# Attention and a gated MLP on one core: combined weights for all 768-token blocks are made in the plain blocks

## The chip, the cores and the metric

The kernel runs on one core of one Trainium2 chip. The time is the device time of one execution in microseconds (us), and lower is better. Five engines work beside each other: TensorE (PE, matmuls; PEld is its weight load), VectorE (DVE), ScalarE (ACT), GpSimd (POOL), and SyncE (SP), which issues nearly all transfers. Each engine takes its own instructions in the order that was fixed when the program was built, and waits on semaphores for the others.

## The reference

```python
k_p = k.reshape(B, H, Sp, pool, D).mean(axis=3)        # 576 keys pooled to 72
v_p = v.reshape(B, H, Sp, pool, D).mean(axis=3)
scores = scale * np.matmul(q, k_p.transpose(0, 1, 3, 2))
attn = softmax(scores)
x = np.matmul(attn, v_p)                               # then (B*S, H*D) = 4608 x 512
h = x @ w_in                                           # 512 -> 2048
g = h * np.clip(h + 3.0, 0.0, 6.0) / 6.0
out = g @ w_out                                        # 2048 -> 512
```

Batch and heads are 8 each, head size is 64, all in float32. Every float32 operand of a large matmul is split into a high and a low part in a reduced type (`hi` is a rounding copy on ACT, `lo = x - hi` on DVE), and a product is three matmuls: hi·hi, hi·lo and lo·hi.

## The kernel before

**Blocks.** The 4608 tokens are cut into blocks (`BLOCKS`): 512, 256, 384 and 384 tokens, and then eight of 384 that are taken two at a time, as four blocks of 768. The first four (blocks 0 to 3) are "plain", the four others use a product scheme with seven block products in place of eight. Attention for a later block runs in small steps ("slots") between the matmuls of an earlier one, so that its PE work is spread over all stages.

**A plain block** (`run`, class `Step`) has 16 steps, one for each 128 of the 2048 hidden columns. Step u does the 12 matmuls of h (L847), then ACT's relu (L855), DVE's `gate` (L859), ACT's `ghi` (L863) and DVE's `glo` (L867), then the `out` products (L878) of step u - 2, three per 128 tokens, and last the hooks of u: calls listed in a table `hooks[block][u]`. The h sums alternate between two PSUM banks, so h of step u + 2 waits for gate of step u. The buffer `g` exists once, so relu of a step waits for `glo` of the one before. All weights are in SBUF in these blocks, each in its own place: tile `w_f` holds the two parts of w_in and w_out of step f. The places lie in two pools, `consts[0]` for f under 8 and `consts[1]` for the others.

**A 768-token block** (`super_block`) treats h as a 2 x 2 block product: x (two token halves by two halves of the 512 columns) times pairs of w_in tiles, done by seven products per pair (`N1`, L1140). Its operands are sums of blocks. The sums of x are made by `x_ops` (eleven makes, each with one DVE operation at L1044 or L1052). The sums of w_in are the same for all tokens: `sums_of(i, h)` makes them once for pair i of 8, in two halves h of 128 columns, in `hooks[2]` and `hooks[3]` at every second step, into a tile `wq` of which there is one buffer; they are stored to DRAM (`w_dram`, shown as wd) by SP. `plain_of` stores the weights that go in as they are (24 stores to wd, 32 to `w2_dram`, shown as w2d); its calls stand in the hooks of blocks 2 and 3, but nothing holds them there.

The weights then stream back for each 768-token block in chunks of 512 KB through two rings, wsFalse and wsTrue (`chunk`, L998). The ring wsFalse lies in the pool `late0`, which takes the place of `consts[0]` at step 9 of block 3 (`swap`); wsTrue lies in `late2`, which takes the place of the pool that holds `wq`, at the last step of block 3 (`more`).

The out part of the second, third and fourth 768-token block (`SEVEN = (1, 2, 3)`) is done by seven products too (`out_seven`, L1267): 28 rounds, each of 18 matmuls of 256 columns. The first does it plainly (`out_plain`, L1194), 16 rounds of 18 matmuls of 512 columns, and beside it `combine` makes the sums of w_out for the others from the chunks that pass (per pair: two adds L1023, four mixes L1026, one ACT copy L1028, one subtraction L1029) and stores them to `w2t_dram` (w2t, L1032).

**What sets the order.** For the first stretch (to step 3 of block 1) the order on every engine is a written table, `ORDER`. Behind it a planner orders the instructions of each engine by a simulated time, in the order of the program among those that it thinks ready. Two helpers bind it: `behind(a, b)` keeps a after b on one engine, with no wait, and `after_mark()` keeps the instruction just written behind the last marked one on its engine; on DVE in plain blocks that is `glo`. Both set only the earliest place. `CUTS` is the share of the attention steps of a 768-token block that goes to its h part, the rest goes to its out part.

Of the kernel before, what the change touches and what calls it, by code (L numbers as in the profile page):

```python
# [8 lines left out]
F32 = mybir.dt.float32  # L9
F32R = mybir.dt.float32r  # L10
# [88 lines left out]
def attention_moe_kernel(  # L99
# [506 lines left out]
    def x_tile(j, name, dtype):  # L606
        if (j, name) not in xs:
            if name == "x":
                xs[j, name] = pool.tile([P, NCC, TMAX], dtype, name=name, bufs=2)
            else:  # L610
                xs[j, name] = early_x[-1].tile(
                    [P, NCC, max(BLOCKS) if j < 2 else TMAX], dtype, name=name, bufs=1
                )
        return xs[j, name][:, :, : BLOCKS[j]]
# [324 lines left out]
    def sums_of(i, h):  # L939

        half = slice(h * P, (h + 1) * P)
        t = early_x[-1].tile([P, 2, 4, P], F32, name="wq", bufs=1)
        hi, q = t[:, 0], t[:, 1]
        for r, w in enumerate(pair_of(i)):
            nc.vector.tensor_tensor(
                out=q[:, 2 * r : 2 * r + 2], in0=w[:, 0, :, half], in1=w[:, 1, :, half], op=ALU.add
            )
            after_mark()
        for to, a, b, how in ((0, 0, 2, ALU.subtract), (2, 2, 3, ALU.add), (3, 3, 0, ALU.subtract), (1, 1, 3, ALU.subtract)):
            nc.vector.tensor_tensor(out=q[:, to], in0=q[:, a], in1=q[:, b], op=how)  # L950
        nc.scalar.copy(hi.bitcast(F32R), q)
        nc.vector.tensor_tensor(out=q.bitcast(F32R), in0=q, in1=hi, op=ALU.subtract)
        for o, at in {7: 0, 3: 1, 5: 2, 6: 3}.items():
            nc.sync.dma_start(dram_of(i, o)[:, :, half], t[:, :, at])  # L954

    def store(to, src):
        nc.sync.dma_start(to, src)  # L957

# [10 lines left out]
    def chunks_of(n):  # L969
        if n not in SEVEN:  # L970
            plain = [w2_dram[f // 4][:, f % 4].rearrange("p q m c -> p (q m c)") for f in range(NF)]
        else:
            plain = []
            for o in KINDS:
                for m in range(NF // 4):
                    if o in RAW2:
                        r, q = RAW2[o]
# [601 lines left out]
```

## Time and profile before

| | us |
|---|---|
| median of 3 runs (lowest to highest) | 889.77 (889.12 to 890.1) |
| the profiled execution | 887.96 |
| span of its profile | 886.2 |

The busy time of every engine over the stages of the kernel is the first thing to read, since a mean over the span hides what bounds each stage. From it one goes to the chain of waits (which line's matmuls the end hangs on, and how long they take one after the other without a break), to the waits of PE (what it stood still for) and of SP (what held up transfers), and to the timeline of DVE between two steps of a plain block. The blocks lie in the span as follows: block 0 to about 128, block 1 to 192, block 2 to 272, block 3 to 344 us, then the 768-token blocks, each first h and then out: 344 to 420 and 491, to 564 and 629, to 698 and 764, to 823 and the end. In block 3, gate of step 4 starts at 292.2, of step 9 at 315.1 and of step 15 at 340.9.

### The profile page before, as it was taken

Reading aid. Unit: us, or ns where it says so; the run is one execution under the profiler, and the core shown is the slowest. Engines: PE = TensorE matmul, PEld = TensorE weight load, DVE = VectorE, ACT = ScalarE, POOL = GpSimd, SP = SyncE. Lnnn points to the kernel's source line nnn. Section 1 sums busy time; section 2 is a strip of 40 time slices with the busy share of each in tenths; the row PEclk is TensorE's granted clock in tenths of the full one; section 3 lists DMA queues with packets and bytes.
Section 4 is the critical chain, followed back from the end, with each engine's and each line's share of the span. In section 5 each row is a group of like instructions: output and inputs, shape, how many; then the busy total and the mean of one; then the engine's idle time right before and its main releaser. Section 6 shows DMA issues by size and latency. Waiting matters only on the chain.

```text
span 886.2 us, 15640 instructions
## 1 busy us (share of the span) xinstructions
PE 867.3 (98%) x5360; PEld 810.2 (91%) x5360; DVE 665.9 (75%) x1340; ACT 555.4 (63%) x1515; POOL 83.1 (9%) x168
## 2 busy tenths in 40 slices
PE   7999999999999999999999999999999999999998
PEld 6788888988989999899888999899999999999998
DVE  6999864567776885879779588997588877466664
ACT  5998766655666665778444678765576846355442
POOL 4100002110111100102000101100110200000000
PEclk9999999999999999999999999999999999999999
DMA  9970205995425144997587978877886777877874
GB/s 302 391 291 1 72 24 194 369 334 150 122 81 158 51 143 130 344 341 253 172 255 238 373 245 278 277 255 231 285 301 213 241 235 239 279 252 239 269 264 131
DMA packets 124654, 200.00 MB, mean 226 GB/s; under 512 B 13216, under 2 KB 81056, under 8 KB 124576
## 3 DMA queue, kind: packets, MB, share of 16 engines
q1 hardware_dynamic: 124432, 199.00, 68.1%
q8 instruction: 43, 0.70, 0.3%
q14 instruction: 35, 0.29, 0.1%
q10 hardware_dynamic: 144, 0.00, 0.0%
HBM read 158.08 MB, written 40.89 MB: 225 GB/s over the span
## 4 chain that ended last, share of the span: by engine, by line
PE 82%; DVE 6%; DMA 4%; ACT 3%; SPq 2%; issue 1%; POOL 0%; DVEq 0%; ACTq 0%
PE psx L1140 23%; PE psx L1267 20%; PE pso L878 12%; PE psh L847 11%; PE psx L1194 8%; PE psa L647 4%; PE psa L464 3%; DMA qt<-q_l 1%; PE psa L573 1%; DMA wd<-wq 1%; ACT e L473 1%; DMA wsFalse<-wd 1%; SPq L957 1%; DMA kst<-k_l 1%; SPq L954 1%
## 5 line engine op out<-in xcount | busy, mean ns | idle before, releaser
L1140 PE MATMUL psx<-x,wsFalse 128*128 128x384 f32 x768 | 150.2, 339 | 3.4 <-DVE g L1104 1.4
L847 PE MATMUL psh<-xhi,w 128*128 128x384 f32 (+2 forms) x520 | 146.1, 340 | 0.1
L1140 PEld LDWEIGHTS psx<-x,wsFalse 128*128 128x128 f32 x768 | 132.8, 188 | 5.3 <-DVE g L1104 1.8
L1119 ACT CAST part<-g 128x768 fp32r<-128x768 f32 x100 | 83.6, 840 | 77.4 <-PE psx L1267 59.7
L1121 DVE TENSOR_TENSOR part<-g,part 128x768 fp32r<-128x768 f32 x100 | 95.4, 956 | 42.1 <-ACT part L1119 42.0
L878 PE MATMUL pso<-w,ghi 128*128 128x512 f32 x384 | 120.6, 399 | 0.4 <-ACT o L883 0.4
L1140 PE MATMUL psx<-x,wsTrue 128*128 128x384 f32 x576 | 115.2, 340 | 1.3 <-DMA wsTrue<-wd 0.7
L1267 PE MATMUL psx<-wsFalse,part 128*128 128x256 f32 x864 | 108.4, 282 | 0.4 <-ACT kept L1242 0.4
L1267 PEld LDWEIGHTS psx<-wsFalse,part 128*128 128x128 f32 x864 | 105.1, 188 | 1.0 <-ACT kept L1242 1.0
L1140 PEld LDWEIGHTS psx<-x,wsTrue 128*128 128x128 f32 x576 | 99.6, 188 | 2.6 <-DMA wsTrue<-wd 1.1
L847 PEld LDWEIGHTS psh<-xhi,w 128*128 128x128 f32 x520 | 93.2, 188 | 7.5 <-DVE g L859 0.4
L473 ACT ACTIVATE e<-psa,mx 128x72 f32<-128x72 f32 x256 | 79.2, 326 | 30.1 <-DVE mx L468 27.3
L502 POOL TENSOR_TENSOR a<-e,sm 128x256 f32<-128x256 f32 x60 | 39.8, 664 | 504.9 <-DVE sm L491 415.3
L847 PE MATMUL psh<-xlo,w 128*128 128x384 f32 (+2 forms) x260 | 87.1, 336 | 0.0
L1267 PE MATMUL psx<-wsTrue,part 128*128 128x256 f32 x648 | 80.6, 281 | 0.0
L878 PEld LDWEIGHTS pso<-w,ghi 128*128 128x128 f32 x384 | 68.9, 188 | 11.0 <-ACT o L883 0.7
L1267 PEld LDWEIGHTS psx<-wsTrue,part 128*128 128x128 f32 x648 | 78.7, 188 | 0.0
L1096 ACT ACTIVATE r<-g,small 128x384 f32<-128x384 f32 x96 | 58.7, 623 | 29.1 <-DVE g L1104 28.6
L1104 DVE TENSOR_TENSOR g<-psx,c 128x384 f32<-128x384 f32 x96 | 52.3, 553 | 30.7 <-PE psx L1140 20.4
L878 PE MATMUL pso<-w,glo 128*128 128x512 f32 x192 | 74.5, 398 | 0.0
L1098 DVE SCALAR_TENSOR_TENSOR g<-r,g 128x384 f32<-128x384 f32 x96 | 55.4, 588 | 10.7 <-ACT r L1096 10.4
L1113 ACT COPY c<-psx 128x384 f32<-128x384 f32 x96 | 45.2, 484 | 28.0 <-PE psx L1140 27.6
(140 smaller groups left out, 1474.8 us busy)
## 6 DMA issues: line engine op xcount, KB each, us to landing
wsFalse<-wd SPq DMA_DIRECT2D x64, 512.0 KB, 4.9
wsTrue<-wd SPq DMA_DIRECT2D x48, 512.0 KB, 5.1
wsFalse<-w2d SPq DMA_DIRECT2D x31, 512.0 KB, 5.1
wsFalse<-w2t SPq DMA_DIRECT2D x27, 512.0 KB, 4.8
wsTrue<-w2d SPq DMA_DIRECT2D x21, 512.0 KB, 5.0
wsTrue<-w2t SPq DMA_DIRECT2D x21, 512.0 KB, 4.8
raw<-w_in_l SPq DMA_DIRECT2D x16, 512.0 KB, 8.5
raw<-w_out_l SPq DMA_DIRECT2D x16, 512.0 KB, 9.1
```

Of the source, the lines that this page charges most:

```text
L473: nc.scalar.activation(self.e[:, h], self.ps[:, h], AF.Exp, bias=self.mx[:, h : h + 1], accum_out=self.sm[:, h : h + 1])
L847: nc.tensor.matmul(self.ps, l[f][:, c, :], r[:, c, :], start=c == 0 and i == 0, stop=c == NCC - 1 and i == 2)
L878: nc.tensor.matmul(pos, l, r, start=f == 0 and i == 0, stop=f == NF - 1 and i == 2)
L1096: nc.scalar.activation(r, src, AF.Relu, bias=half_low, scale=GSCALE / (6.0 * WSCALE))
L1098: nc.vector.scalar_tensor_tensor(out=g_of[i][:, k], in0=r, scalar=GSCALE, in1=src, op0=ALU.min, op1=ALU.mult)
L1104: nc.vector.tensor_tensor(out=g_of[i][:, k], in0=ps, in1=kept, op=ALU.add)
L1113: nc.scalar.copy(c, ps)
L1119: nc.scalar.copy(t[:, 0], src)
L1121: nc.vector.tensor_tensor(out=t[:, 1], in0=src, in1=t[:, 0].bitcast(F32), op=ALU.subtract)
L1140: nc.tensor.matmul(ps, w[:, l, c * P : (c + 1) * P], t[:, r, c], start=o in (1, 2, 5) and c == 0 and k == 0, stop=c == 1 and k == 2, skip_ ...
L1194: nc.tensor.matmul(to, l, w[:, qs, r], start=f == 0 and k == 0, stop=end and k == 2)
L1267: nc.tensor.matmul(to, t[:, l, k, i * P : (i + 1) * P], w[:, k, r], start=begin and k == 0 and y == 0 and i % 2 == 0, stop=m == NM - 1 and ...
```

## The change

All four 768-token blocks do out by seven products. `out_plain`, `combine` and their tables go; `out_seven` becomes `out_of`, called for each. The sums of w_out are made in block 3 by the new `sums_of_out`, from the weights in SBUF. The sums of w_in come earlier: pairs 0 to 2 in block 1, whole (256 columns); pairs 3 to 6 in block 2 in halves; pair 7 in block 3, whole. Each make is in two parts one step apart: adds, mixes and the ACT copy in the one, subtraction (in two instructions) and stores in the other. Those of block 3 go into rooms of their own: the tiles `w_f` of steps that are through. The plain stores are put behind the third w_in sum's stores on SP. The high and low parts of block 1's x share one tile, so that the other's place holds the sums of block 1. `CUTS` of the first 768-token block goes from .85 to .7.

```diff
-SEVEN = (1, 2, 3)
-MAKE = (range(8), (), (), ())
-TURN = (0, 2, 4, 6, 7, 9, 10, 12)
-CUTS = (.85, 0.85, 0.85, 0)
-TAIL = 5
+CUTS = (.7, 0.85, 0.85, 0)
...
+            elif j == 1:
+                t = early_x[-1].tile([P, 2, NCC, max(BLOCKS) // 2], dtype, name="x01", tag="xhi", bufs=1)
+                xs[j, "xhi"], xs[j, "xlo"] = t[:, 0], t[:, 1]
...
+    def sums(blocks, mixes, hi, q):
+        for r, (high, low) in enumerate(blocks):
+            nc.vector.tensor_tensor(out=q[:, 2 * r : 2 * r + 2], in0=high, in1=low, op=ALU.add)
             after_mark()
+        for to, a, b, how in mixes:
             nc.vector.tensor_tensor(out=q[:, to], in0=q[:, a], in1=q[:, b], op=how)
+            after_mark()
         nc.scalar.copy(hi.bitcast(F32R), q)
+    def low_of(hi, q):
+        for x in (slice(0, 2), slice(2, 4)):
+            nc.vector.tensor_tensor(out=q[:, x].bitcast(F32R), in0=q[:, x], in1=hi[:, x], op=ALU.subtract)
+            after_mark()
+    def room(f):
+        if f:
+            t = const(f).tile([P, 2, 4, 2 * P], F32, name="wq", tag=f"w_{f}")
+            return t[:, 0], t[:, 1]
+        return (
+            early_x[-1].tile([P, 4, 2 * P], F32, name="wq", bufs=1),
+            const(0).tile([P, 4, 2 * P], F32, name="wq", tag="w_0_0"),
+        )
+    def sums_of(i, at, place):
+        hi, q = place()
+        blocks = [(w[:, 0, :, at], w[:, 1, :, at]) for w in pair_of(i)]
...
+        def rest():
+            low_of(hi, q)
+            for o, x in {7: 0, 3: 1, 5: 2, 6: 3}.items():
+                for m, t in enumerate((hi, q)):
+                    nc.sync.dma_start(dram_of(i, o)[:, m, at], t[:, x])
+            staged.append(traced[-1].name)
+        return rest
+    def sums_of_out(i, place):
+        hi, q = place()
+        blocks = [w_of[2 * i + r, 1].bitcast(F32).rearrange("p m (q c) -> p m q c", q=2) for r in range(2)]
...
+        def rest():
+            low_of(hi, q)
+            for m, t in enumerate((hi, q)):
+                nc.sync.dma_start(w2t_dram[i // 2][:, :, i % 2, m], t)
+        return rest
...
     def store(to, src):
         nc.sync.dma_start(to, src)
+        behind(traced[-1], staged[2])
...
-        (out_seven if n in SEVEN else out_plain)(n, j, bank, parts, split_g, split_f, pairs, second_att, rest, last_h)
+        out_of(n, j, bank, parts, split_g, pairs, second_att, rest, last_h)
...
-    make = [lambda i=i, h=h: sums_of(i, h) for i in range(NPR) for h in range(2)]
+    every, halves = slice(0, 2 * P), [slice(h * P, (h + 1) * P) for h in range(2)]
+    hooks = {1: {}, 2: {}, 3: {}}
+    def in_two(j, u, make):
+        rest = []
+        hooks[j].setdefault(u, []).append(lambda: rest.append(make()))
+        hooks[j].setdefault(u + 1, []).insert(0, lambda: rest.pop()())
+    for i, u in enumerate((4, 7, 10)):
+        in_two(1, u, lambda i=i: sums_of(i, every, lambda: early_room(2 * P, "xlo")))
+    for n in range(8):
+        in_two(2, 2 * n, lambda n=n: sums_of(3 + n // 2, halves[n % 2], lambda: early_room(P, "wq")))
...
-    for n, step in enumerate(make):
-        hooks[2 + n // NPR].setdefault(2 * (n % NPR), []).append(step)
+    in_two(3, 0, lambda: sums_of(NPR - 1, every, lambda: room(0)))
+    for i, (u, f) in enumerate(((2, 0), (4, 1), (5, 2), (6, 3), (7, 4), (8, 5), (10, 8), (12, 9))):
+        in_two(3, u, lambda i=i, f=f: sums_of_out(i, lambda: room(f)))
```

More of the change, by code (lines that the diff above doesn't have):

```diff
@@ new lines, in sums_of_out @@
+    def sums_of_out(i, place):
+        hi, q = place()
+        blocks = [w_of[2 * i + r, 1].bitcast(F32).rearrange("p m (q c) -> p m q c", q=2) for r in range(2)]
+        sub, add = ALU.subtract, ALU.add
+        sums([(w[:, 0], w[:, 1]) for w in blocks], ((3, 3, 1, sub), (1, 1, 0, sub), (0, 0, 3, add), (2, 2, 0, sub)), hi, q)
+        def rest():
[3 more added lines that the diff above has]
+        return rest
@@ L1003, in attention_moe_kernel @@
         first_of.append(len(chunks))
[L1004 removed]
+        chunks += chunks_of()
     def next_w(n, m):
@@ L1162, in super_block @@
         att_banks[:] = ["a0", "a1"]
-        (out_seven if n in SEVEN else out_plain)(n, j, bank, parts, split_g, split_f, pairs, second_att, rest, last_h)
+        out_of(n, j, bank, parts, split_g, pairs, second_att, rest, last_h)
         assert not rest
-    def out_plain(n, j, bank, parts, split_g, split_f, pairs, att, rest, last_h):
-        NT2 = 2 * HALF // P
-        paced = Paced(att, NT2 * (NF - TAIL))
-        split_f(0)
-        banks = ["o0", "h0", "o2", "o1", "h1", "o3"]
-        sums, outs = {}, []
-        for f in range(NF):
-            if f + 1 < NF:
-                split_f(f + 1)
-            w = next_w2(n, f)
-            for i in MAKE[n]:
-                if f == TURN[i]:
-                    combine(n, i)
-            for t in range(NT2):
-                if f < NF - TAIL:
-                    paced.slot()
-                elif rest:
-                    rest.pop(0)()
-                hi, lo = (parts[f][:, m].rearrange("p h t -> p (h t)")[:, t * P : (t + 1) * P] for m in range(2))
-                products = (hi, 0), (hi, 1), (lo, 0)
-                end = f == NF - 1
-                if f == 0:
-                    sums[t] = [(slice(0, 2), bank(banks, t, DM))]
-                    if n == len(supers) - 1 and t == NT2 - 1:
-                        sums[t] = [(slice(0, 1), sums[t][0][1][:, :256]), (slice(1, 2), bank(["a0"], 0, 256))]
-                for qs, pos in sums[t]:
-                    for k, (l, r) in enumerate(products):
-                        to = pos.rearrange("p (q c) -> p q c", c=DM // 2)
-                        nc.tensor.matmul(to, l, w[:, qs, r], start=f == 0 and k == 0, stop=end and k == 2)
-                        if f == 0 and k == 0:
-                            behind(traced[-1], last_h)
-                if not end:
-                    continue
-                if t % 3 == 0:
-                    o3 = late[1].tile([P, 4 * HALF], F32, name="o", tag="part", bufs=3)
-                o = o3[:, t % 3 * DM : (t % 3 + 1) * DM]
-                at = starts[j] + t * P
-                for x, (qs, pos) in enumerate(sums[t]):
-                    cols = slice(qs.start * 256, qs.stop * 256)
-                    (nc.vector.tensor_copy if (t + x) % 2 else nc.scalar.copy)(o[:, cols], pos)
-                    nc.sync.dma_start(out[at : at + P, cols], o[:, cols])
-            if f == NF - TAIL - 1:
-                paced.upto(len(paced.steps))
@@ L1210, in out_seven, with out_of @@
-    def out_seven(n, j, bank, parts, split_g, split_f, pairs, att, rest, last_h):
+    def out_of(n, j, bank, parts, split_g, pairs, att, rest, last_h):
         NT2, NM, W2 = HALF // P, NF // 4, DM // 2
```

66 lines of the change are left out of this document (16 added, 50 removed).

## The prediction

> **What bounds the kernel now.** I read the page first, then the busy time by stretches cut at the stage borders, then the chain of waits, then the waits by engine, and last the timeline around the places that the change touches.
>
> ```profile
> span 886.2 us, 15640 instructions
> PE 867.3 (98%) x5360; PEld 810.2 (91%) x5360; DVE 665.9 (75%) x1340; ACT 555.4 (63%) x1515; POOL 83.1 (9%) x168
> ...
> core 0: us, PE busy (x) PEld busy (x) DVE busy (x) ACT busy (x) POOL busy (x), PEclk, DMA share, GB/s
> 128.00:192.00 64.00, 63.80 (x404) 57.90 (x403) 35.76 (x97) 40.15 (x153) 12.30 (x25) 1.00 0.82 278
> 192.00:272.00 80.00, 78.06 (x417) 69.53 (x417) 62.47 (x170) 46.93 (x157) 9.51 (x19) 1.00 0.43 124
> 272.00:343.90 71.90, 71.90 (x389) 65.89 (x388) 55.43 (x130) 43.74 (x130) 6.73 (x14) 1.00 0.41 123
> ...
> 419.70:491.40 71.70, 71.70 (x331) 58.68 (x331) 57.90 (x102) 31.80 (x59) 2.38 (x6) 1.00 0.72 230
> ...
> 563.90:628.90 65.00, 64.80 (x537) 64.59 (x536) 53.01 (x80) 36.74 (x70) 2.36 (x5) 1.00 0.80 262
> 698.50:763.70 65.20, 64.99 (x540) 64.79 (x539) 48.24 (x68) 34.13 (x61) 2.58 (x4) 1.00 0.77 249
> ```
>
> The rows are blocks 1, 2 and 3 (plain), then the out part of the first block of 768 tokens (plain), of the second and of the third (by seven). PE has work in 98% of the span at a granted clock of 1.00, so the time is PE's work plus its few gaps. A change pays if it takes matmul time away, and costs if it makes PE wait. VectorE (DVE), at 75%, is what can make it wait.
>
> **The change part by part.**
>
> *Out of the first 768-token block by seven products.* Issue times come from long unbroken pieces of the chain, counts from the two matmul lines.
>
> ```profile
> 463.05 28.71 PE psx L1194 x123
> ...
> 745.48 13.52 PE psx L1267 x112
> ...
> 822.73 59.17 PE psx L1267 x498
> ...
> L1194 PE MATMUL psx<-wsFalse,part x180: 392/395/477, 419.9 to 491.4; 128*128 128x512 f32 x180
> L1194 PE MATMUL psx<-wsTrue,part x108: 392/395/419, 439.8 to 483.0; 128*128 128x512 f32 x108
> ...
> L1267 PE MATMUL psx<-wsFalse,part x864: 277/280/388, 564.0 to 882.3; 128*128 128x256 f32 x173
> L1267 PE MATMUL psx<-wsTrue,part x648: 277/280/377, 566.9 to 878.1; 128*128 128x256 f32 x162
> ```
>
> Plain: 180 + 108 = 288 matmuls of 512 columns at 28.71/123 = 0.2334 us: 67.2 us. By seven: (864 + 648)/3 = 504 of 256 columns, at 13.52/112 = 0.1207 us (0.1188 in the last stage, which has no attention beside it): 60.8 or 59.9 us. Saved 6.4 to 7.3 us. The rows of whole stages say 71.7 against 65.0 and 65.2, so 6.6 us. I take **-6.6**, ends -5.9 and -7.3. DVE is no obstacle there: it needs 53.0 of 65.0 us in the second block, doing what the first will then do.
>
> The Trainium skill speaks against this term: "TensorE: Matmul & The Clock Gate", section "Back-to-back issue gap", gives a sustained 81 ns per matmul of 128 columns and 131 ns of 512. A straight line between them, an estimate, puts 256 columns at about 98 ns; by it 504 of them cost 49.4 us against 37.7 for 288 long ones, and the change would lose 11.7 us in this stage. The rows above disagree: 256 columns take 0.52 times what 512 take.
>
> *CUTS .7.* The first block's h part hands 15% of the attention steps of blocks 6 and 7 to its out part. Both are full of PE work, so it moves time and takes none: 0.
>
> *Combined w_out weights leave the out part and come to block 3.* Each of the eight makes is two adds, four mixes, one ACT copy and one subtraction. The DVE rows of the three lines over the out part (the other row is empty):
>
> ```profile
> 420.00:492.00 72.00, 10.33 (x16) 1.00 0.72 231
> ...
> 420.00:492.00 72.00, 12.47 (x32) 1.00 0.72 231
> ...
> 420.00:492.00 72.00, 9.62 (x8) 1.00 0.72 231
> ```
>
> The sixteen adds, 32 mixes and eight subtractions take (10.33 + 12.47 + 9.62)/8 = 4.05 us of DVE per make: 2.85 for adds and mixes, 1.20 for the subtraction, which the change puts one step later. Now block 3: all of DVE and the part of the w_in sums (tile wq) in steps 4 to 8 and in steps 9 to the end.
>
> ```profile
> 292.20:315.10 22.90, 22.90 (x123) 20.92 (x123) 18.26 (x49) 14.56 (x47) 1.92 (x4) 1.00 0.25 69
> 315.10:340.90 25.80, 25.80 (x135) 23.56 (x134) 21.17 (x39) 13.88 (x23) 0.99 (x2) 1.00 0.40 127
> ...
> 292.20:315.10 22.90, 7.04 (x20) 1.23 (x2) 1.00 0.25 69
> 315.10:340.90 25.80, 6.02 (x16) 1.85 (x3) 1.00 0.40 127
> ```
>
> Without w_in sums, steps 4 to 8 hold 18.26 - 7.04 = 11.2 us of DVE. The change hooks five makes on them: five first parts and four second parts, 5 x 2.85 + 4 x 1.20 = 19.1. Together 30.3 us in a stretch of 22.9: DVE falls 7.4 us behind, or 8.4 with a gap of 0.2 us a step between gate and lo that nothing fills (my choice: a third of the 0.58 in the row of lo below). Steps 9 on: 21.17 - 6.02 = 15.2, and 3 x 1.20 + 2 x 2.85 = 9.3 of makes: 24.5 of 25.8, so hardly any of it is caught up. How late may DVE be before PE stops? One place shows it, where operations for the x of the next block held the gate up (rows of ACT, DVE and PE; behind them an undisturbed lo, and DVE with its w_in part around the held gate):
>
> ```profile
> 319.49 0.58 ACT L855 ACTIVATE g<-psh,small 128x384 f32<-128x384 f32 x1
> ...
> 323.04 0.55 DVE L859 SCALAR_TENSOR_TENSOR g<-g,psh 128x384 f32<-128x384 f32 x1
> ...
> 325.36 0.43 PE L847 MATMUL psh<-xhi,w 128*128 128x384 f32 x1
> ...
> 311.01 0.56 DVE L867 TENSOR_TENSOR glo<-g,ghi 128x384 fp32r<-128x384 f32 x1 [0.58 <-ACT ghi L863]
> ...
> 315.10:328.10 13.00, 13.00 (x71) 11.99 (x70) 12.78 (x19) 8.36 (x13) 0.99 (x2) 1.00 0.60 203
> ...
> 315.10:328.10 13.00, 1.54 (x4) 0.62 (x1) 1.00 0.60 203
> ...
> DVE wq L945 <- DMA wd<-wq: 14.2, 11, 2.8
> ```
>
> The gate could start at 320.07, starts at 323.04, ends at 323.59; PE needs its PSUM bank at 325.36 and doesn't wait. So 2.97 + 1.77 = 4.7 us of lateness are free. Taking 8.4, PE loses 8.4 - 4.7 = 3.7. I take **+3.7**. Ends: 0, if DVE spreads the makes over its free time; and about +10.6, if the whole 0.58 us stays open in all five steps (+1.9), the x operations still run where they do now, ahead of the gate, where DVE is full (12.78 of 13.0) and the makes of steps 9 to 11 would come on top (2 x 1.20 + 2.85 - 1.54 = +3.7), and DVE enters step 4 late, because step 2 reuses the room of step 0 and waits for its stores (14.2/11 = +1.3, as the w_in sums do now). What queues behind a late make on DVE is gate and lo of the next step, and behind them relu (it writes the buffer that lo reads), h two steps on and out.
>
> ACT gets nine copies for eight of half the size in block 3:
>
> ```profile
> L1028 ACT CAST th<-tq x5: 1052/1055/1060, 427.8 to 485.1; 128x1024 fp32r<-128x1024 f32 x5
> ...
> L951 ACT CAST wq<-wq x16: 610/624/662, 201.6 to 346.0; 128x512 fp32r<-128x512 f32 x16
> ```
>
> 9 x 1.06 - 8 x 0.62 = 4.5 us more, hidden in ACT's free 71.9 - 43.7 us. The 16 stores (128 x 4 x 256 words, 8.4 MB in all) move with them to a stretch whose DMA share is 0.41; they go to rooms of their own in dead weights, so the next make seldom waits for them. On SP they stand between the loads of block 3; SP waits there for DVE as it does now.
>
> *w_in sums earlier, in two parts.* Three pairs go to block 1, four stay in block 2, one goes to step 0 of block 3. Block 1 gets 3 x 4.05 = 12.2 us of DVE on 35.8 of 64.0, spaced three steps apart: hidden, and 0 to +2 if not. Their stores are halved in size and become 96 instead of 64. Before, SP was stuck behind them at the end of block 3, and PE paid for it (PE's waits after 340, then SP's rows):
>
> ```profile
> PE psx L1140 <- DMA wsFalse<-wd: 1.2, 1, 1.2
> PE psx L1140 <- DMA wsTrue<-wd: 0.7, 1, 0.7
> ...
> 331.93 17.41 SPq L954 DMA_DIRECT2D wd<-wq  x12
> ...
> 350.94 1.54 SPq L998 DMA_DIRECT2D wsTrue<-wd  x3
> ```
>
> The last sums' stores are issued until 349, and only then can the pool that holds them be given up and the first chunks for the second ring (wsTrue) be loaded. With the last of them in step 3 these 1.9 us go. What is late next is the x of the first 768-token block, whose operations now stand behind the makes: 0 to 2, I take 0.5. Net **-1.4**, ends -2.4 and +0.5.
>
> *Plain stores behind the third w_in sum.*
>
> ```profile
> L957 SPq DMA_DIRECT2D w2d<-w x32: 437/711/1402, 148.7 to 195.7; - x32
> L957 SPq DMA_DIRECT2D wd<-w x24: 427/724/1002, 146.8 to 190.3; - x24
> ```
>
> 56 stores of 128 x 2 x 256 words, 14.7 MB, fill the DMA from 147 to 196. The third sum's stores go out near 177, so most of the 56 move by some 30 us into block 2, which moves 124 GB/s: 9.9 MB and some 11 more in 80 us is 260 GB/s, less than the 278 of block 1 now. The queue in block 2 also holds the q, k and v loads and eight sums with one buffer, whose reuse already waits 14.2 us for stores. PE's gaps there (80.0 - 78.1 = 1.9 us in the row of block 2) may go or come again later. I take 0, ends -1.9 and +4. Sharing one tile between both parts of block 1's x: both are written after the last h of block 0 now too: 0, at most +1.
>
> **Sum.** -6.6 + 3.7 - 1.4 = **-4.3 us**. The profiled execution took 887.96 us for its span of 886.2, the median of the runs is 889.77, 1.8 more. So 883.7 by the profiled one, and **885.5** by the median, on which the rest is counted.
>
> **The rivals.**
>
> *DVE in block 3 is never late enough.* For: it has free time before step 4, a make has no upper limit to its place, and it may slide into gaps after step 11. Against: 30.3 us in 22.9. Then -8.0: 881.8. Chance 0.25.
>
> *DVE is the bound of block 3, and the time ends on the other side.* One engine in order with gate and lo behind the makes; at +10.6 the sum is +2.6: 892.4. It decides from a stall of 8.0 us on, and can be told from 9.8 on. For: the x operations stand between lo and gate today, ahead of a gate that could run. Against: PE has 4.7 us of room, and x operations have their place in the program after the makes. Chance 0.16.
>
> *Block 2 is clogged by the plain stores.* Sums wait longer for their buffer, loads for attention land late; +4: 889.5. For: in block 1 these stores took the DMA share to 0.82, in block 2 it starts from 0.43 and more depends on its loads. Against: they ran beside loads already, and PE lost 1.9 us. Chance 0.11.
>
> *It doesn't do what it says:* seven products save nothing, since they need a rate of 0.1334 us, which no stretch of three stages shows. 892.1, chance 0.01. The Trainium skill's rule above would be worse still; the trace doesn't bear it out.
>
> *The forecast*, a stall of 1 to 8 us: 0.47. Its own range is 883 to 889.8.
>
> **How the numbers follow.** A measurement of this kernel tells 0.2%, about 1.8 us, from no change: below 888.0 is faster, above 891.5 slower. Faster: 0.25 and 0.39 of the forecast's 0.47: 0.64. Same: 0.08 of the forecast, 0.09 of the clogged block 2: 0.17. Slower: 0.16 + 0.02 + 0.01 = 0.19. The range runs from the first rival with some of block 2's gaps gone too (881.8 - 1.5 = 880.3) to a stall of 9.5 us (891.3); above it lie about 0.12, below about 0.05.
>
> **What would show it.** Out of the first 768-token block at 64 to 67 us with 504 matmuls; if 71, the first term is wrong. Steps 4 to 8 of block 3 at 25 to 28 us with DVE near full and PE waiting for DVE g; with PE still full the first rival holds, with 10 us of such waits the second. At 344 to 370 no wait for wsTrue; a wait for x instead is the price of late x operations. In block 2 PE's gaps stay at some 2 us; 5 or more speak for the clog. I am wrong most easily in the stall, since the order on DVE is made by a planner and isn't in the diff.

## The result and the profile after

The changed kernel takes **905.57 us** (median of 5 runs, 904.84 to 908.43) against 889.77 (888.84 to 891.62) in the same comparison: ratio 1.0175, 95% interval 1.0159 to 1.0192. It is slower by 15.8 us; the prediction was 885.5, its range ended at 891.3.

First the busy time by stretches, cut at the same events in both kernels (first gate of block 1, of block 2, of block 3, last gate of block 3, first and last out matmul of the first 768-token block). Columns: stretch, its length, busy PE, PEld, DVE, ACT, POOL (number of instructions), granted clock, DMA share, GB/s. Before:

```profile
130.30:192.20 61.90, 61.70 (x392) 56.01 (x390) 33.62 (x94) 38.55 (x145) 10.99 (x24) 1.00 0.85 288
192.20:274.00 81.80, 79.86 (x430) 71.42 (x429) 62.35 (x170) 48.72 (x162) 9.51 (x19) 1.00 0.44 125
274.00:340.90 66.90, 66.90 (x362) 61.42 (x361) 53.00 (x124) 40.43 (x118) 6.73 (x14) 1.00 0.40 120
340.90:419.90 79.00, 76.47 (x447) 73.52 (x446) 61.30 (x152) 59.92 (x198) 12.81 (x24) 1.00 0.86 288
419.90:491.80 71.90, 71.90 (x332) 58.84 (x331) 57.70 (x102) 31.96 (x58) 2.18 (x6) 1.00 0.72 231
```

After:

```profile
span 903.4 us, 16224 instructions
...
130.30:190.80 60.50, 60.50 (x388) 55.23 (x388) 44.90 (x124) 43.16 (x159) 12.40 (x26) 1.00 0.53 165
190.80:278.20 87.40, 82.34 (x421) 73.12 (x419) 55.56 (x151) 43.65 (x140) 8.09 (x17) 0.96 0.74 230
278.20:367.40 89.20, 79.14 (x391) 69.48 (x391) 76.01 (x168) 48.44 (x131) 7.00 (x14) 0.94 0.56 182
367.40:444.20 76.80, 72.72 (x430) 70.27 (x429) 61.24 (x147) 58.07 (x201) 12.87 (x23) 1.00 0.81 266
444.20:510.50 66.30, 66.09 (x558) 65.89 (x557) 52.41 (x79) 35.70 (x71) 3.66 (x8) 1.00 0.78 251
```

The out part gained what it should, 71.9 to 66.3. Block 2 lost 5.6 and block 3 22.3 us. In the middle three rows PE is idle 19.2 us against 4.5 before, and the granted clock, 1.00 before, is 0.96 and 0.94: 0.04 x 87.4 + 0.06 x 89.2 = 8.9 us of full speed are missing. 14.7 + 8.9 make up most of the 25.7 us that these three stretches grew. A part of a stretch's growth is work that stood in another one before (block 3 holds 391 matmuls for 362), so idle PE and missing clock are the better measure: 3.1 + 3.5 us more in block 2, 10.1 + 5.4 in block 3.

**Block 2.** The timeline (start, duration, what ran; in brackets the idle time before it and what ended it), SP, ACT and PE, and then the two stretches around the stop:

```profile
192.73 2.62 SPq L998 DMA_DIRECT2D w2d<-w  x4
195.40 2.48 SPq L998 DMA_DIRECT2D wd<-w  x3
...
199.48 1.86 SPq L998 DMA_DIRECT2D w2d<-w  x3
201.39 2.67 SPq L998 DMA_DIRECT2D wd<-w  x3
204.16 0.76 SPq L881 DMA_DIRECT2D out<-o  x1
...
209.22 0.60 ACT L880 ACTIVATE o<-pso 128x512 f32<-128x512 f32 x1 [8.91 <-DMA out<-o]
...
209.88 1.22 PE L875 MATMUL pso<-w,ghi 128*128 128x512 f32 x2 [3.21 <-ACT o L880]
...
206.60:210.00 3.40, 0.19 (x2) 0.13 (x1) 0.00 (x0) 0.60 (x1) 0.00 (x0) 0.86 0.53 155
210.00:216.00 6.00, 6.00 (x15) 4.71 (x16) 4.64 (x12) 3.53 (x9) 0.00 (x0) 0.51 0.98 320
```

A store of block 1's output stands on SP behind the plain stores (L998), so its buffer `o` comes free late, ACT stands still for 8.9 us, and PE for 3.2. Then, with PE full of work, the clock is 0.51 for six us. The plain stores, held back until the third w_in sum, now go close together, from 184 to 244 us (called one run below), and what stands among them on SP waits for those ahead of it: 24 of the 56 go before this store. The DMA is full meanwhile; the same stretch in the changed kernel and in `paced`, a run below that spreads these stores out:

```profile
192.00:204.00 12.00, 12.00 (x66) 11.11 (x65) 7.92 (x22) 5.08 (x12) 0.00 (x0) 1.00 1.01 325
```

```profile
192.00:204.00 12.00, 12.00 (x66) 11.12 (x64) 9.14 (x26) 6.65 (x16) 0.86 (x2) 1.00 0.33 101
```

The mean share of block 2, 0.74, hides this. But a full DMA isn't the price by itself: before the change the same stores filled it from 147 to 196 us (1.03 to 1.06), and PE lost about 1 us there.

**Block 3**, cut at the gates of the steps 6 and 11; then, from DVE's timeline, adds and subtractions of sums:

```profile
278.20:308.90 30.70, 29.62 (x167) 27.00 (x168) 19.49 (x55) 16.54 (x61) 2.79 (x6) 1.00 0.45 134
308.90:346.00 37.10, 30.67 (x140) 26.40 (x138) 36.56 (x81) 19.69 (x54) 3.96 (x8) 0.91 0.42 139
346.00:367.40 21.40, 18.84 (x86) 16.08 (x86) 19.96 (x34) 12.21 (x19) 0.26 (x1) 0.92 0.98 324
...
282.99 0.76 DVE L939 TENSOR_TENSOR wq<-w 128x256 f32<-128x256 f32 x2 [1.52 <-DMA out<-o]
294.40 0.76 DVE L939 TENSOR_TENSOR wq<-w 128x256 f32<-128x256 f32 x2 [2.72 <-DMA wd<-wq]
307.16 1.29 DVE L948 TENSOR_TENSOR wq<-wq 128x512 fp32r<-128x512 f32 x2 [3.43 <-ACT wq L944]
312.60 1.53 DVE L939 TENSOR_TENSOR wq<-w 128x512 f32<-128x512 f32 x2
315.84 1.28 DVE L939 TENSOR_TENSOR wq<-w 128x512 f32<-128x512 f32 x2
318.74 1.28 DVE L939 TENSOR_TENSOR wq<-w 128x512 f32<-128x512 f32 x2
320.74 1.28 DVE L939 TENSOR_TENSOR wq<-w 128x512 f32<-128x512 f32 x2
322.61 1.28 DVE L939 TENSOR_TENSOR wq<-w 128x512 f32<-128x512 f32 x2
326.12 1.28 DVE L939 TENSOR_TENSOR wq<-w 128x512 f32<-128x512 f32 x2
```

Two halves of w_in's sums (128x256), hooked on block 2, run at 283 and 294, the sum of the last pair ends only at 308, and then six makes of w_out (adds 128x512) begin within 14 us, though they are hooked on steps 2 to 8. DVE has 11.2 us free in the first stretch and 0.5 in the second, where PE stands still for 6.4 us and runs at 0.91.

### The profile page after: what moved, and what is told of

Same layout as the page of the kernel before. It is cut to its first block, busy times and chain, and to the rows that moved or that the text cites. A ratio compares the mean times of both kernels' runs of the same rounds, so it can differ in the third digit from the quotient of the medians.

```text
span 903.4 us, 16224 instructions
## 1 busy us (share of the span) xinstructions
PE 869.7 (96%) x5576; PEld 821.8 (91%) x5576; DVE 687.3 (76%) x1365; ACT 562.9 (62%) x1528; POOL 84.3 (9%) x168
## 4 chain that ended last, share of the span: by engine, by line
PE 68%; DVE 14%; DMA 7%; ACT 5%; SPq 4%; issue 2%; POOL 0%; DVEq 0%; ACTq 0%; POOLq 0%
PE psx L1238 26%; PE psx L1155 22%; PE pso L875 7%; PE psh L844 7%; PE psa L644 3%; PE psa L460 2%; DVE wq L942 2%; DVE wq L939 2%; DVE wq L948 2%; SPq L998 2%; DMA wd<-wq 1%; ACT e L469 1%; DVE g L856 1%; PE psa L569 1%; DMA kst<-k_l 1%
## 5 line engine op out<-in xcount | busy, mean ns | idle before, releaser
L1137 ACT CAST part<-g 128x768 fp32r<-128x768 f32 x112 | 93.6, 837 | 82.5 <-PE psx L1238 76.7
L1238 PE MATMUL psx<-wsFalse,part 128*128 128x256 f32 x1152 | 143.3, 282 | 0.0
L1139 DVE TENSOR_TENSOR part<-g,part 128x768 fp32r<-128x768 f32 x112 | 106.5, 954 | 47.3 <-ACT part L1137 47.0
L1238 PEld LDWEIGHTS psx<-wsFalse,part 128*128 128x128 f32 x1152 | 139.6, 188 | 0.0
L844 PE MATMUL psh<-xhi,w 128*128 128x384 f32 (+2 forms) x392 | 121.2, 364 | 5.6 <-DVE g L856 5.6
L1238 PE MATMUL psx<-wsTrue,part 128*128 128x256 f32 x864 | 109.4, 282 | 0.6 <-ACT kept L1213 0.6
L1238 PEld LDWEIGHTS psx<-wsTrue,part 128*128 128x128 f32 x864 | 105.4, 188 | 1.4 <-ACT kept L1213 1.4
L844 PEld LDWEIGHTS psh<-xhi,w 128*128 128x128 f32 x392 | 73.6, 192 | 13.6 <-DVE g L856 7.2
L875 PEld LDWEIGHTS pso<-w,ghi 128*128 128x128 f32 x384 | 71.7, 195 | 15.0 <-ACT o L880 3.5
L844 PE MATMUL psh<-xlo,w 128*128 128x384 f32 (+2 forms) x196 | 70.5, 360 | 0.1
```

Source lines behind the costliest of these rows:

```text
L844: nc.tensor.matmul(self.ps, l[f][:, c, :], r[:, c, :], start=c == 0 and i == 0, stop=c == NCC - 1 and i == 2)
L875: nc.tensor.matmul(pos, l, r, start=f == 0 and i == 0, stop=f == NF - 1 and i == 2)
L1137: nc.scalar.copy(t[:, 0], src)
L1139: nc.vector.tensor_tensor(out=t[:, 1], in0=src, in1=t[:, 0].bitcast(F32), op=ALU.subtract)
L1238: nc.tensor.matmul(to, t[:, l, k, i * P : (i + 1) * P], w[:, k, r], start=begin and k == 0 and y == 0 and i % 2 == 0, stop=m == NM - 1 and ...
```

## Experiments

Two explanations are at stake: the amount of the makes' work on DVE in block 3, and the plain stores in one run, which hold up block 2 and push the makes together. The letters of the theories are those of each run's own expectation and change their meaning from run to run. A planner orders the instructions anew after every edit, so each run was read in its trace before it was taken as an answer. Every ratio is to the kernel before on the same chip.

### No order for the plain stores: free_stores, free_pool

```diff
     def store(to, src):
         nc.sync.dma_start(to, src)
-        behind(traced[-1], staged[2])
```

> The changed kernel, with the one line gone that keeps the plain stores behind the third w_in sum on SP. Theory A (the order): in the changed kernel the w_in sums of block 2 wait for their stores behind the plain stores, so that the first w_out make gets its room only at step 6 or 7 of block 3, and all makes fall on DVE in one stretch of some 38 us; without the line the makes are spread over steps 0 to 14, PE loses at most 8 us in block 3, and the time is 886 to 894. Theory B (the amount): DVE has 76 us of work for 71 us in block 3 in any order; the time stays at 898 to 906.

919.8 us, ratio 1.0349 (1.0328 to 1.0369). Both theories missed. Block 3 did shorten, 76.0 us from first to last gate, but between the last gate of block 1 and the first of block 2 lie 37.4 us (3.0 in the changed kernel): `xlo` of block 2 takes the tile that held block 1's sums of w_in and waits for the last stores out of it, which stand on SP behind plain stores until 206.8 us, and PE's weight loads wait 15.6 us for `xlo`. Held back or not, the plain stores end up ahead of something on SP.

> As free_stores, and the adds and mixes of the w_out makes run on GpSimd (idle for 65 of 72 us in block 3) in place of DVE; DVE keeps the subtractions (8 x 1.2 us). If DVE is what holds block 3 once the order is mended, this is faster than free_stores by what block 3 still loses there: 880 to 885 (theory A) against free_stores; by theory B it is the one that helps, 882 to 888, while free_stores does not. If GpSimd slows DVE beside it, or the late subtractions hold up the x operations of the first 768-token block, 886 to 892.

This is the same with adds and mixes of w_out on GpSimd: 920.04, 1.0345 (1.0327 to 1.0364), outside all its ranges; block 3 76.9 us. No gain, and a part of the reason stands in DVE's groups in 60 us of block 3, first with GpSimd adding (free_pool), then without (free_stores):

```profile
L864 DVE TENSOR_TENSOR glo<-g,ghi 128x384 fp32r<-128x384 f32 x12 | 10.3, 862 | 3.1 <-ACT ghi L860 3.1
L856 DVE SCALAR_TENSOR_TENSOR g<-g,psh 128x384 f32<-128x384 f32 x12 | 6.6, 552 | 5.8 <-ACT g L852 5.8
```

```profile
L864 DVE TENSOR_TENSOR glo<-g,ghi 128x384 fp32r<-128x384 f32 x11 | 6.1, 553 | 0.3 <-ACT ghi L860 0.2
L856 DVE SCALAR_TENSOR_TENSOR g<-g,psh 128x384 f32<-128x384 f32 x11 | 6.1, 550 | 0.6 <-ACT g L852 0.6
```

`glo`, with two operands in SBUF, takes 862 ns instead of 553; the gate, with one of them in PSUM, the same 550. What GpSimd takes over, DVE pays back in part. Still DVE is busy for 57.8 us of block 3, against 70.8 in free_stores, and block 3 is no shorter: the amount on DVE alone doesn't set its length there. With GpSimd a mix takes 906 ns, on DVE 430, so each make takes longer; what of this holds block 3 wasn't tried.

### Plain stores a few at a time: paced, paced85

```diff
-        behind(traced[-1], staged[2])
+        behind(traced[-1], staged[-1])
```

Each plain store waits for the sum that is the last one made where it is written, so the 56 go between the sums, not in one run.

> The changed kernel, but each plain store stands behind the latest w_in sum's stores before it in the program (staged[-1] in place of staged[2]), so that they are spread over blocks 2 and 3 and not sent off in one go. Nothing else differs, and DVE has the same work; in the order of DVE the adds of the w_out makes then begin in every step from 1 to 12 of block 3, where in the changed kernel six of them begin in steps 7 and 8. Theory D (the plain stores in one go are the root: they hold up the out store of block 1 and the w_in sums' stores of block 2, and through their one buffer the makes of block 3): the wait of PE for ACT o near 207 goes, block 3 takes 72 to 78 us from gate 0 to gate 15 in place of 89, and the time is 884 to 891. Theory B (the amount of DVE work holds block 3 whatever the order): block 3 stays at 83 to 90, the time at 898 to 905.

891.11, ratio 0.9997 (0.9981 to 1.0014), at the edge of theory D's 884 to 891: **14.5 us of the loss go with one index** (theory D: the plain stores in one go are the root). Block 2 is 85.0 us and block 3 77.5; PE waits nowhere for `o`. But it isn't faster than the kernel before, so something else takes back what the seven products save.

> As paced, with CUTS of the first 768-token block back at .85. If the move of attention steps between its two parts costs nothing, the time is that of paced within 1.5 us; if the out part by seven products is short of DVE or ACT time, it is faster than paced, and if the h part is, slower.

With CUTS at .85 again 892.21, 1.0011 (0.9997 to 1.0026): the cut costs nothing that can be told.

### The out stores on another queue: out_act2

```diff
-                nc.sync.dma_start(out[at : at + P], o)
+                (nc.scalar if blk.j else nc.sync).dma_start(out[at : at + P], o)
```

> The changed kernel, but the out stores of the blocks 1 to 3 are issued from ScalarE's queue instead of SyncE's, so that they no longer stand behind the plain stores. In the changed kernel the third out store of block 1 stands on SP at 204.16 us among the plain stores, ScalarE waits 8.9 us for its buffer, PE 3.2 us for ScalarE, and the granted clock is 0.5 for the 6.9 us that follow. Theory C (this one chain is what the plain stores cost at the border of blocks 1 and 2): the wait of 3.2 us and the 3.45 us lost to the half clock go, PE waits nowhere for o, 897 to 901 us. Theory B (the plain stores hold the sums' stores and the loads as well, so PE runs dry there for another reason): 903 to 908 us. The crowd of makes in block 3 is the same in both, 85 to 90 us from first to last gate.

(A first form, out_act, which moved block 0's stores too, gave no time.) 903.43, 1.0152 (1.0138 to 1.0165), 2.1 us less than the changed kernel: theory B. PE waits there all the same, now

```profile
214.80 1.65 PE L875 MATMUL pso<-w,ghi 128*128 128x512 f32 x3 [5.50 <-ACT ghi L860]
```

and by the profile the reason is ACT itself, which issues its store (ACTq) only when a plain store's transfer is through and stands still for 8.7 us until then:

```profile
213.81 0.34 ACTq L881 DMA_DIRECT2D out<-o  x1
214.24 0.51 ACT L860 CAST ghi<-g 128x384 fp32r<-128x384 f32 x1 [8.73 <-DMA w2d<-w]
```

So it isn't SP's order alone: the store waits for a plain transfer on another queue too. Why it has to isn't shown, and neither is how much of the wait in the changed kernel is SP's order and how much the full DMA. Taking one store out of the line doesn't do; breaking up the run does (paced).

### Without the sums of w_out: no_make, paced_no_make

```diff
-        hi, q = place()
...
-        sums([(w[:, 0], w[:, 1]) for w in blocks], ...)
...
-            low_of(hi, q)
-            for m, t in enumerate((hi, q)):
+            for m, t in enumerate(blocks):
```

> The changed kernel, but the sums of w_out are not computed: the stores to w2t take plain weights from SBUF, in number and size as before, and DVE and ACT do nothing for them. It leaves out the DVE and ACT work of the eight makes. Both theories: block 3 is as short as in the kernel before (gate 0 to gate 15 in 67 us, +-3), and the time is 881 to 887, so the makes cost some 20 us. If block 3 stays over 75 us, it isn't DVE that holds it (theory C: the transfers of block 3).

907.18, 1.0216 (1.0192 to 1.0240): missed as a time, though block 3 was 69.7 us, as both theories had it. The second is the same with the paced stores.

> The kernel with each plain store behind the sums staged last (measured 891.1 and 892.2 with the two cuts; here the cut .85), but the sums of w_out are not computed in block 3: what is stored in their place are the uncombined weights, in the same eight places with as many bytes. It prices the sums alone, with the plain stores out of the way. Theory A (the amount of the eight makes on VectorE is what block 3 costs, 77.7 us from first to last gate against 67.0 before): block 3 falls to 67 to 70 us and the time to 881 to 885 us, below the kernel before by the 6 us of the seven products and the earlier sums of w_in. Theory B (the length of block 3 comes from the stores and the held clock, not from VectorE): block 3 stays over 74 us, 888 to 892 us.

899.12, 1.0089 (1.0064 to 1.0114): block 3 fell to **67.0** us, the least that theory A allowed, but the time missed, since between blocks 1 and 2 were 21.8 us where paced85 has 3.0. DVE's timeline of paced_no_make and then of paced85:

```profile
194.22 1.29 DVE L948 TENSOR_TENSOR wq<-wq 128x512 fp32r<-128x512 f32 x2 [0.66 <-ACT wq L944]
199.66 1.97 DVE L623 TENSOR_TENSOR xlo<-x,xhi 128x384 fp32r<-128x384 f32 x4 [3.21 <-DMA wd<-wq]
```

```profile
179.64 1.28 DVE L948 TENSOR_TENSOR wq<-wq 128x512 fp32r<-128x512 f32 x2
186.22 1.97 DVE L623 TENSOR_TENSOR xlo<-x,xhi 128x384 fp32r<-128x384 f32 x4 [0.87 <-ACT xhi L622]
```

The third sum ends 15 us later, and block 2's xlo needs its tile and waits for its stores. This second toll at the same border (21.7 us in no_make) isn't time that the makes take: it comes with the new order on DVE, and it spoils these two times as prices of anything.

### More pairs in block 1: four, paced_four, eight, lighter

```diff
-    for i, u in enumerate((4, 7, 10)):
+    for i, u in enumerate((4, 7, 10, 13)):      # four, paced_four
+    for i, u in enumerate((4, 6, 8, 10)):       # eight: and no sum of w_in in block 3
+    for i, u in enumerate((4, 6, 8)):           # lighter: ten halves in block 2, four stores a sum
```

> The changed kernel, with four pairs of w_in in block 1 and three in block 2 (six halves) in place of three and four; plain stores as in the changed kernel. The chain of w_in sums ends earlier, and the makes of w_out begin in steps 1 to 12 of block 3, although the plain stores still go in one go. Theory D splits here: the wait near 207 stays (some 3 us of PE and what the lower clock adds), block 3 falls to 72 to 78; 889 to 895. Theory B: 898 to 906.

> Both edits. Theory D: as paced or 1 to 2 us better, since both take away the same bunch; 883 to 890. Theory B: 898 to 905.

> The kernel with each plain store behind the sums staged last, the cut .85, and one pair of w_in more made in block 1: four pairs there at steps 4, 6, 8 and 10 instead of three at 4, 7 and 10 (the last at the same step as before), so that block 2 makes the pairs 4 to 7 in its eight halves and block 3 has only the eight makes of w_out, none of w_in (nine makes before). In block 1 VectorE is busy 44.9 us of 60.5, so a fourth make of some 4.5 us fits there. Theory A (block 3 is bound by the amount on VectorE): block 3 is shorter by 2 to 4 us than the 77.7 of the run with the cut .85, 887 to 890 us, a little below the kernel before. Theory B (the four makes in a row hold the one tile of block 1 longer by their stores, so block 2's rest tile xlo waits for them, as at 17.5 us of border in the run with a fourth pair at step 13): 893 to 900 us with a wait of PE for xlo.

917.11 (1.0284, 1.0260 to 1.0309), 899.96 (1.0090, 1.0065 to 1.0116) and 902.06 (1.0124, 1.0103 to 1.0146). All three pay the same toll: 21.5, 17.5 and 17.2 us between the blocks. As times, four missed both theories, paced_four fell into theory B's range by luck (its block 3 is 75.3 us, where B means 83 to 90), and eight lies 2 us above theory B, whose wait for `xlo` it shows. In eight the adds of the third and the fourth sum begin at 171.6 and 185.5: a sum with its stores holds the tile for some 14 us, so a fourth isn't through when block 2 wants it.

> Each plain store behind the sums staged last, the cut .85, and the sums of w_in out of block 3: three pairs in block 1 at steps 4, 6 and 8 (before 4, 7 and 10, so that the third is done well before block 2 takes its tile), the other five in block 2 in ten halves (before eight halves, and the last pair in block 3), high and low parts of a product stored in one transfer (four stores a sum, before eight). Block 3 then has eight makes on VectorE instead of nine. The two runs of this arrangement with nine makes measured 891.1 and 892.2 us, block 3 77.7 us from first to last gate; without the eight sums of w_out block 3 was 67.0 us, so a make costs some 1.3 us of block 3. Theory A (the amount on VectorE is what is left): block 3 75 to 77 us, the border of blocks 1 and 2 3 to 5 us, and SP has some 20 us less to issue: 887 to 891 us. Theory B (the ten halves slide into block 3, as eight did in the changed kernel, and crowd the makes there): block 3 over 80 us, 894 to 902 us.

890.08, 0.9989 (0.9975 to 1.0004): theory A's time. Block 3 is 71.5 us, shorter than it said, and the border 6.4, longer, but its step 12 is 12.0 long, and SP stands behind the stores of the last make, so PE waits 4.0 us for wsTrue afterwards.

### The same with earlier makes, and one edit undone: early_makes, early_go

```diff
-OUT3 = ((2, 0), (4, 1), (5, 2), (6, 3), (7, 4), (8, 5), (10, 8), (12, 9))
+OUT3 = ((2, 0), (3, 1), (4, 2), (5, 3), (6, 4), (7, 5), (8, 6), (10, 8))
```

> As the run with the sums of w_in out of block 3 (890.1 us, the same as before; block 3 71.4 us from first to last gate, but step 12 of it 12 us long, and then a wait of PE of 4.0 us for wsTrue, whose loads stand on SP behind the stores of the last make), with the eight makes of w_out one step earlier each: at steps 2, 3, 4, 5, 6, 7, 8 and 10 instead of 2, 4, 5, 6, 7, 8, 10 and 12, so that they end ahead of the ten operations that split the first 768-token block's input at steps 11 to 14. Nothing is left out. Theory A (what was left of the loss is where the last two makes stand, on VectorE among the splits and on SP ahead of the loads): block 3 70 to 72 us with no step over 9 us, no wait for wsTrue, the h part back to 75 to 78 us from 83: 882 to 887 us, below both kernels. Theory B (the amount costs the same wherever it stands): the steps 3 to 9 lengthen by as much as step 12 shortens, 888 to 893 us.

890.23, 0.9991 (0.9978 to 1.0004): theory B. Step 12 is 6.5 us and the wait for wsTrue is gone, but steps 4 to 8 take 5.6 to 6.7 each; the amount costs about the same wherever it stands. early_go is this kernel with the plain stores in one run again (`staged[2]`).

> The kernel of the run early_makes with one edit undone: the plain stores stand behind the third w_in sum, as in the changed kernel, not behind the sums staged last, so that they go in one run of about 50 us on SP in block 2. Theory D (the run of plain stores is a cost of its own): PE waits in block 2 for a sum's or an output's tile, the granted clock is 0.5 behind it, halves of block 2 slide into block 3 again, and the time is 6 to 14 us above the run early_makes. Theory E (it only mattered by pushing the makes of block 3 together, which now have more room): within 3 us of it.

901.63, 1.0125 (1.0110 to 1.0140), **11.4 us more for that one edit**: theory D. ACT's row and PE's of early_go, and behind them its block 2 as a stretch:

```profile
214.33 0.60 ACT L882 ACTIVATE o<-pso 128x512 f32<-128x512 f32 x1 [12.82 <-DMA out<-o]
...
214.98 1.22 PE L877 MATMUL pso<-w,ghi 128*128 128x512 f32 x2 [7.85 <-ACT o L882]
...
192.00:282.20 90.20, 80.87 (x419) 71.68 (x417) 56.34 (x157) 43.57 (x138) 7.38 (x15) 0.96 0.73 227
```

The same stretch of early_makes:

```profile
192.20:275.60 83.40, 81.91 (x450) 74.38 (x448) 65.14 (x184) 49.12 (x159) 7.72 (x15) 1.00 0.61 178
```

PE stands 7.9 us for `o`, the clock drops, and DVE gets 8.8 us less done in block 2; in block 3 it is then busy for 75.2 us, against 67.5.

### One part at a time: win_only, win_paced, makes_only

win_only is the kernel before with the sums of w_in and the plain stores as in the change; win_paced has the plain stores paced; makes_only is win_paced with the makes in block 3 and without `combine`, out of the first 768-token block still by plain weights:

```diff
-MAKE = (range(8), (), (), ())
+MAKE = ((), (), (), ())
...
+    for i, (u, f) in enumerate(((2, 0), (4, 1), (5, 2), (6, 3), (7, 4), (8, 5), (10, 8), (12, 9))):
+        in_two(3, u, lambda i=i, f=f: sums_of_out(i, lambda: room(f)))
```

> The kernel before, with only the w_in sums moved (pairs 0 to 2 in block 1, in two parts) and the plain stores behind the third of them; the first 768-token block does out plainly and makes the sums of w_out there, as before. This measures the other half of the change alone. Theory A and B: blocks 1 and 2 lose some 4 us, as in the changed kernel, the start of the first 768-token block wins 1 to 2; 889 to 893. If it is 900 or more, the loss isn't in the w_out makes.

> The kernel before with only the sums of w_in as in the change (three pairs in block 1, eight halves in block 2, the last pair in block 3) and each plain store behind the sums staged last; the first 768-token block does out by plain weights and makes the combined ones there, as before. Its orders on VectorE are those of the run with the cut .85 (892.2 us) but for the eight makes in block 3, which it does not have. Theory A (the eight makes are what block 3 lost): block 3 67 to 69 us from first to last gate against 77.7, and the whole is the kernel before plus the step of my sum on the earlier sums of w_in alone, -3 to +1 us: 887 to 891 us. Theory B (block 3 is long without the makes too, by w_in's last pair or the stores): block 3 over 73 us, 893 us or more.

> As the run win_paced, with the eight makes of w_out in block 3 as in the change, at the same steps, and none in the first 768-token block's out, which still goes by plain weights. It differs from the run with the cut .85 (892.2 us) only in that out part: 288 products with 512 columns here, 504 with 256 there. Theory A (the sum of my prediction was right term by term but for the size of the makes): the seven products are worth 5.5 to 6.6 us, so 897 to 899 us here, and the makes cost 8 to 11 us against win_paced. Theory B (out by plain weights without its makes is faster too, so that the seven were worth less): under 895 us.

896.72 (1.0089, 1.0069 to 1.0109), 892.80 (1.0031, 1.0017 to 1.0046) and 898.66 (1.0098, 1.0073 to 1.0123). DVE has the same order in blocks 1 to 3 of makes_only and paced85; win_paced agrees with them up to block 3, where a few operations change places besides the makes. Block 3 from first to last gate, one row of each of the three in this order:

```profile
275.50:344.80 69.30, 67.02 (x349) 60.91 (x348) 39.80 (x81) 35.40 (x102) 7.28 (x14) 0.98 0.59 199
```

```profile
275.90:353.10 77.20, 71.43 (x366) 64.00 (x365) 69.12 (x144) 43.33 (x110) 7.99 (x14) 0.98 0.87 287
```

```profile
274.60:352.30 77.70, 71.22 (x366) 64.00 (x365) 69.14 (x146) 43.37 (x111) 8.00 (x14) 0.98 0.86 285
```

The makes put 29.3 us more on DVE and 7.9 more on block 3. Of the 7.9 us, 4.4 are PE work: 17 matmuls more stand in block 3 (366 for 349), and from its last gate to the end the profiled executions take 542.3 us for 546.8. PE's idle time grows by 3.5 us, and PE waits 4.3 us for DVE's gates, where it waited for none before. With the makes alone the time is 5.9 us above win_paced, less than the 8 to 11 expected, and with the seven products it comes down again by 6.4, to the 892.2 of paced85. So theory A holds for the seven products, and for block 3 but for 0.3 us (69.3, where it allowed 67 to 69). But win_paced itself is 2.8 us above the kernel before, where A allowed at most 1, and win_only, above the range of both theories, has another 3.9: the run of plain stores, where no makes of w_out stand in block 3 to be pushed together.

### Fewer instructions for the same sums: fewer

```diff
-        for x in (slice(0, 2), slice(2, 4)):
-            nc.vector.tensor_tensor(out=q[:, x].bitcast(F32R), in0=q[:, x], in1=hi[:, x], op=ALU.subtract)
+        nc.vector.tensor_tensor(out=q.bitcast(F32R), in0=q, in1=hi, op=ALU.subtract)
...
-((3, 3, 1, sub), (1, 1, 0, sub), (0, 0, 3, add), (2, 2, 0, sub))
+((slice(3, 0, -2), slice(3, 0, -2), slice(1, None, -1), sub), (0, 0, 3, add), (2, 2, 0, sub))
```

> The kernel of the run early_makes (890.2 us, ratio 0.9991) with fewer instructions for the same sums, nothing left out: the subtraction that gives the low part is one instruction instead of two, and the first two mixes of a w_out make are one instruction over two of the four products (the second is read before it is written). Per make of w_out six instructions instead of eight, by the rows of free_stores 2 x 0.711 - 1.20 = 0.2 us and 2 x 0.421 - 0.687 = 0.16 us less VectorE time, 2.9 us over eight makes. Theory A (block 3 is bound by the amount on VectorE): block 3 shrinks by 2 to 3 us from 72.6, 887 to 889 us, below the kernel before by 0.2 to 0.4%. Theory B (PE loses by the chains of dependent steps, add to mix to copy to subtraction, which stay as long): within 1 us of early_makes, 889.5 to 891.5.

892.10, 1.0016 (0.9998 to 1.0033): neither shown. The new order puts ten operations for x into one step of 10.8 us, ahead of a gate that PE waits for, and block 3 is 71.2 us instead of 72.6. Whether the rest of the makes' price is DVE's time or their chains of dependent steps stays open. No version beat the kernel before by more than can be told.

## Why the prediction was wrong

From run to run the medians step as follows: +2.8 (win_paced against before) + 5.9 (makes_only against win_paced) - 6.4 (paced85 against makes_only) - 1.1 (paced against paced85: the cut) + 14.5 (the changed kernel against paced) = 15.7, of 15.8 measured. Each run starts where the one ahead of it ends, so the steps have to add up to the whole; that they do proves nothing, and other orders of the edits would share it out otherwise. The kernel before itself was 889.0 to 891.1 in the eight comparisons, so each step that spans two of them is good to some 1 to 2 us: taken against each comparison's own kernel before, the -6.4 is -7.0, the +14.5 is +15.3, and win_only against win_paced, 3.9 by medians, is 5.0.

| step of the prediction | said | measured |
|---|---|---|
| out of the first 768-token block by seven | -6.6 (-7.3 to -5.9) | -5.6 in the trace, -6.4 by medians (4.7 between the out parts of makes_only and paced85) |
| CUTS .7 | 0 | -1.1, not told from 0 |
| makes of w_out in block 3 | +3.7 (0 to +10.6) | +5.9 |
| w_in sums earlier | -1.4 (-2.4 to +0.5) | +2.8, with the plain stores spread over blocks 2 and 3 |
| plain stores behind the third sum | 0 (-1.9 to +4) | +14.5 |

**Right to about 1 us**: the first term, with its 504 matmuls in 66 us. The 5.6 us lie just under its least end, 5.9, which the working doesn't derive; the row holds 54 other matmuls, for 44 before. Without the makes of w_out beside it the plain out part takes 70.6 us (makes_only), by seven products 65.9 (paced85).

**Right in kind, small in size**: the makes. PE waits for DVE's gates in block 3, as forecast; the free 4.7 us of lateness were read from one place and the rest of the stall was worked out for makes that sit on their hooks. In paced85 they do, but for the first, which is a step late; steps 4 to 8 take 26.5 us (25 to 28 foreseen), and the price is 5.9, between the ends. The changed kernel, where they don't, takes 35.0. (9 x 1.06 - 8 x 0.62, the extra time of ACT, is 4.6 us and not 4.5; nothing hangs on it.)

**Wrong in sign, as far as the runs tell it**: the earlier sums. The 1.9 us of waits for wsTrue and wsFalse go as foreseen (in the changed kernel 0.5 are left, in win_paced none), but win_paced pays more than that elsewhere: 2.6 us more in block 2 (84.4) and 2.4 in block 3 (69.3), where PE waits 2.3 us for a load of q and the clock is halved behind it. The sum counted the stores as smaller and didn't count that 96 of them, for 64, lengthen the line that this load stands in; in win_paced plain stores stand in that line as well. That the load is late for either reason was not tried by itself.

**The step that failed**: "Plain stores behind the third w_in sum ... I take 0, ends -1.9 and +4." It compared bytes with what the DMA can move, as a mean over 80 us: 260 GB/s against 278. Over the block they did go through (230 GB/s, share 0.74). But while they go, the DMA is full (1.01 in the row above), and over 11 us of queue (192.7 to 204.2 in the rows above) stand ahead of one output store and its buffer. What showed in place of the 0 is 14.5 us. The rival "Block 2 is clogged by the plain stores" had the mechanism and was priced at less than a third of its size. It looked for late sums and loads: the sums were late, and what stopped PE first was an output's store. The prediction's own sign for it, 5 us of PE's gaps in block 2, was met (87.4 - 82.3 = 5.1). And it ended at block 2, while the larger part lies in block 3: late halves of w_in pushed six makes into 14 us. The prediction's own warning, that the planner's order isn't in the diff, was the place; it was taken as a small error of the stall and not as a way in which one term causes another. The three terms don't add: the run of plain stores costs 3.9 us without the makes (win_only against win_paced), 11.4 with early ones, 14.5 in the change.

## What to carry to other kernels

A transfer that is moved is priced by what will stand behind it and whose buffer that holds, and by the DMA's share while it goes, not by its mean over a stage. Work handed to an engine with 17 us free over a stage is not hidden if late arrivals can push it together: look for what sets its start, not for its hooks. Where two edits feed one queue, their prices don't add.

## What was not expected of the hardware

Gaps of PE of little over 2 us were followed by some 3.4 us (in paced, after one of 2.44 us, by nearly 6) at a granted clock of 0.5 with PE fully busy, but not always. In the changed kernel a gap of 2.32 us (PE's row and the stretch behind it):

```profile
328.87 0.69 PE L644 MATMUL psa<-ahi,vhi 128*128 128x384 f32 x1 [2.32 <-DVE arem L595]
...
328.50:332.00 3.50, 3.13 (x10) 2.83 (x11) 3.41 (x9) 1.44 (x3) 1.05 (x2) 0.51 0.44 149
```

In paced85 one of 2.56 us left it at 1.00:

```profile
285.72 0.73 PE L460 MATMUL psa<-kbd,qt 128*128 128x144 f32 x4 [2.56 <-DMA qt<-q_l]
...
286.00:292.00 6.00, 6.00 (x33) 5.33 (x32) 2.96 (x10) 2.94 (x12) 1.86 (x4) 1.00 1.01 338
```

The Trainium skill, "TensorE: Matmul & The Clock Gate", sections "Part 1: The HAM clock gate (the "warmup" mystery)" and "HAM oscillation — how this bites in real kernels", speaks of a free-running activity window of about 3.4 us and warns of gaps over that length. The length of the slow spells agrees; the gaps that set them off here are shorter. So a wait of 2.3 us can cost about 4 (2.32 + 0.49 x 3.5, an estimate from the rows), and the prediction had no term for it.
